# Joint products of k and v for two pairs of heads, with a remade order, in a linear-attention and feed-forward kernel

## The chip, the cores and the metric

The kernel runs on one core of a Trainium2 chip. The metric is the device time of one execution in microseconds (us). TensorE is called PE in the rows of the profile (its weight loads PEld), VectorE DVE, ScalarE ACT, GpSimd POOL and SyncE SP.

## The reference

A linear attention with softmaxes over q's rows and over the sequence of k is followed by a feed-forward net with a squared ReLU; all is float32. There are 8 batches of 8 heads, 576 positions and 64 columns a head; the net has 512 inputs and 2048 hidden units.

```python
q_s = exp(q - max(q, -1));  q_s = q_s / (sum(q_s, -1) + 1e-09)
k_s = exp(k - max(k, 2));   k_s = k_s / (sum(k_s, 2) + 1e-09)
kv = np.einsum('bhsd,bhse->bhde', k_s, v)
attn = np.einsum('bhsd,bhde->bhse', q_s, kv)
x = attn.transpose(0, 2, 1, 3).reshape(4608, 512)
g = np.maximum(x @ w_in, 0.0) ** 2
out = g @ w_out
```

## The kernel before

**Blocks and pairs.** A block is a batch: 512 of its 576 positions, the other 64 going to x_left for the end. Its eight heads are treated as four pairs, written b.pr; two heads of 64 columns fill the 128 partitions. A float32 product with full precision is made of three products of rounded parts (high by high, high by low, low by high), each with 512 moving columns; they are the bulk of PE's work. Blocks 0 to 2 go through the net step by step: one step is one slice of 128 hidden units of one block, with four groups of three products for the hidden layer (tokens h), relu, square, high and low part (relu, rm, ghi, glo), and four output tiles (tokens o). From block 3 on two blocks at a time go through a scheme with seven products (tokens s0, s1, s2; x0 to x2 prepare its inputs), whose weights come through a ring of tiles (tokens R).

**What sets the order.** Each engine runs its instructions in the order in which the kernel issues them. Two strings of tokens state that order: ORDER up to step 17, LIST from there to the end. `run` takes a token of LIST to a function; `kv/3.1` is the token kv of pair 1 of block 3. In LIST the attention of blocks 2 to 7 stands between the tokens of the net.

**The attention of one pair** (`attention`, from block 2 on). k's maximum is made and spread (km, k1, k2), subtracted (ke, on DVE) and exponentiated (kx, on ACT); q likewise (qm, qd, qx, qs, qy), then turned through DRAM (tb, Bw, B). Then come the tokens that the change touches:

- **kv**, on PE, is one *visit*: ten matmuls, five sequence slices of two heads, each 64 stationary columns (k) by 65 moving ones (v and a column of ones for the sum). One head's results go to partitions 0 to 63 of a PSUM bank, the other's to 64 to 127. The trace shows each matmul as two records, 20 to a visit, as `bank<-vt,kt`. With the changed and unchanged pairs there are 24 visits in blocks 2 to 7; for 2.0 and 2.1 they read another tile for k (`bank<-vt,ke`).
- **kr**, on DVE: 1e-9 added to the sum (rs), the reciprocal, and the scaling of the product (kf).
- **kh**, on ACT: the rounded high part is copied into the split operand kvs, by two copies of 64x64 in blocks 3 and 4 (THREE), by four in the others.
- **kl**, on DVE: two subtractions of 64x64 give the low part, also into kvs.
- **kz**, on POOL: two memsets, where kvs changes its layout (ahead of blocks 3 and 5).
- **P0 to P3**, on PE, multiply q by kvs (`bank<-qs,kvs`, 320 and 256 columns; in blocks 3 and 4 P0 and P1 of three matmuls each); **c** and **d** take them out of PSUM.

There are two split operands, used in turn by n % 2, where n counts the pairs; pairs 2.0 and 2.1 both use the first:

```python
kv_split = [const.tile([P, 2, P], F32R, name="kvs")]
kv_split.append(late.tile([P, 2, P], F32R, name="kvs1"))
kvs = kv_split[n % NB if two else 0]
```

The banks of kv and P come from next_bank: two in turn up to block 4, a single one after it.

Of the kernel before, what the change touches and what calls it, by code (L numbers as in the profile page):

```python
# [8 lines left out]
F32 = mybir.dt.float32  # L9
F32R = mybir.dt.float32r  # L10
# [86 lines left out]
kr/2.1 rm20 o.18.2 ke/2.2 kp/2.1 kh/2.1 B/2.2 o.18.3 k2/2.3 h21_0 ghi20 h21_1 kx/2.2 glo20 h21_2 w5.WA qs/2.3 h21_3
o.19.0 relu21 kl/2.1 o.19.1 ke/2.3 rm21 P0/2.1 w6.WA o.19.2 qm/3.0 qy/2.3 c0/2.1 o.19.3 kx/2.3 d0/2.1 h22_0 tb/2.3
ghi21 P1/2.1 h22_1 glo21 qd/3.0 Bw/2.3 c1/2.1 h22_2 d1/2.1 w7.WA qm/3.1 xh0/2.1 h22_3 xl0/2.1 P2/2.1 o.20.0 relu22
w0.a1 Lq/3.2 o.20.1 rm22 w0.s2 o.20.2 c2/2.1 qx/3.0 d2/2.1 XL/2.1 w0.s3 o.20.3 qs/3.0 P3/2.1 w0.s4 h23_0 ghi22  # L100
c3/2.1 h23_1 glo22 qh0/2.2 qy/3.0 h23_2 d3/2.1 h23_3 xh1/2.1 tb/3.0 xl1/2.1 kv/2.2 relu23 qm/3.2 Bw/3.0 ql0/2.2
# [20 lines left out]
ql0/3.3 h34_2 w3.h34 glo33 h34_3 st.1.1 w3.h12 qs/4.2 o.32.0 w3.l12 relu34 o.32.1 st.1.3 rm34 o.32.2 kx/3.3 w3.l34
w3.W12 o.32.3 qm/4.3 qy/4.2 kv/3.3 ghi34 w3.W34 h35_0 glo34 kp/3.3 Lk/4.1 h35_1 tb/4.2 h35_2 kr/3.3 qd/4.3 Lv/4.1
h35_3 k1/4.0 kh/3.3 o.33.0 relu35 w4.a2 o.33.1 k2/4.0 rm35 o.33.2 qx/4.3 B/4.0 w4.s1 o.33.3 qs/4.3 h36_0 ghi35 h36_1
glo35 qy/4.3 Lq/5.1 h36_2 km/4.1 h36_3 o.34.0 kl/3.3 x0.LB11 relu36 ke/4.0 o.34.1 Bw/4.2 rm36 P0/3.3 w4.a1 kx/4.0
o.34.2 tb/4.3 c0/3.3 w4.s2 o.34.3 back.0 w4.s3 k1/4.1 P1/3.3 ghi36 XL/3.3 h37_0 w4.s4 qh0/4.0 h37_1 glo36 c1/3.3
# [15 lines left out]
glo44 h45_3 ke/5.1 o.43.0 x0.LB22 relu45 tb/5.1 o.43.1 rm45 x0.T10 Bw/5.1 o.43.2 kx/5.1 o.43.3 x0.lB110 x0.hT10
h46_0 s0.R.1 ghi45 x0.lT10 h46_1 glo45 qd/5.2 h46_2 km/5.2 x0.hB220 h46_3 back.1 Lq/6.0 o.44.0 x0.T30 relu46 o.44.1
x0.T20 rm46 s0.R.2 o.44.2 x0.hT30 x0.T40 o.44.3 x0.hT20 x0.lT30 h47_0 ghi46 s0.R.3 x0.pB210 h47_1 x0.hT40 glo46
h47_2 x0.hB221 x0.lT20 qx/5.2 h47_3 x0.T11 o.45.0 s0.R.4 relu47 x0.lB111 o.45.1 rm47 x0.T31 o.45.2 x0.hT11 o.45.3
x0.hT31 x0.lT11 B/5.0 o.46.0 ghi47 x0.lT31 o.46.1 glo47 x0.pT40 o.46.2 s0.R.5 o.46.3 x0.T21 s0.0.A11 x0.T41 x0.hT21
x0.lT21 back.2 o.47.0 s0.0.c1 qs/5.2 x0.pB211 ev.2.0.a s0.0.S2 x0.hT41 st.2.0 k1/5.2 x0.pT41 s0.0.A12 s0.0.u2 s0.R.7
k2/5.2 qh0/5.0 x0.pB220 o.47.1 s0.0.r11 s0.0.S3 qh1/5.0 s0.0.m11 x0.pB221 back.3 ev.2.1.d s0.0.h0 s0.0.S1 s0.R.8
s0.0.u3 st.2.1 s0.0.l0 ql0/5.0 o.47.2 s0.0.a22 o.47.3 ev.2.2.a s0.0.A22 ql1/5.0 s0.R.6 s0.0.rf1 ev.2.3.d s0.0.qf1
qm/5.3 st.2.2 P0/5.0 s0.o.0.0 s0.0.r21 qy/5.2 c0/5.0 s0.o.0.1 s0.0.m21 s0.R.9 s0.o.0.2 d0/5.0 s0.0.h1 st.2.3  # L150
s0.o.0.3 s0.0.l1 P1/5.0 tb/5.2 s0.1.A11 s0.R.10 c1/5.0 d1/5.0 qd/5.3 Bw/5.2 s0.0.S4 qm/6.0 XL/5.0 s0.1.c1 ke/5.2
# [161 lines left out]
def attention_ffn_kernel(ctx: ExitStack, tc: tile.TileContext, q, k, v, w_in, w_out, out):  # L313
# [991 lines left out]
```

## Time and profile before

| | us |
|---|---|
| Median of 3 runs (lowest, highest) | 844.3 (843.94, 845.71) |
| The profiled execution, its own time | 843.6 |
| Its span, first to last instruction | 841.8 |
| PE busy | 833.6 |
| DVE busy | 550.4 |
| ACT busy | 494.3 |
| POOL busy | 288.4 |

The span lies 1.8 us under that execution's own time. Matmuls are pipelined, and their ends are modelled; the times from start to start tell the pace better than the durations. A few matmul records are missing from the trace. Nearly all instructions carry one line, L293, that of the helper that issues them, so groups are told apart by the tiles they write and read.

### The profile page before, as it was taken

What the parts mean: (1) busy time and instruction counts of PE and PEld (TensorE: products, weight loads), DVE (VectorE), ACT (ScalarE), POOL (GpSimd) and SP (SyncE); (2) the same over time, 40 slices, a digit from 0 to 9 for tenths busy, and PEclk for the clock granted to TensorE, in tenths of its full rate; (3) what the DMA queues carried; (4) which work ended last, traced back from release to release, by engine and by line L of the source; (5) the groups of instructions that cost most, each with busy time, mean ns of one, the idle gap of its engine ahead of it and who ended that gap; (6) DMA issues with size and microseconds to landing.
All of it is one profiled execution on the core that took longest, in us unless ns stands there. A gap on an engine that the chain in (4) does not pass through costs nothing.

```text
span 841.8 us, 13068 instructions
## 1 busy us (share of the span) xinstructions
PE 833.6 (99%) x4286; PEld 678.3 (81%) x4286; DVE 550.4 (65%) x1153; ACT 494.3 (59%) x934; POOL 288.4 (34%) x275
## 2 busy tenths in 40 slices
PE   8999999999999999999999999999999999999997
PEld 6778787878888888888887888888888888888886
DVE  7898888879988888668887896634348132222321
ACT  4889866677556656567667556566464244444411
POOL 4578654567776645244323143031002100000000
PEclk9999999999999999999999999999999999999999
DMA  9969987965777889988898837765576374554611
GB/s 238 274 182 301 255 289 231 325 189 174 215 225 239 238 252 273 271 240 277 243 252 260 286 113 233 231 202 181 174 236 186 100 225 151 160 170 151 183 62 50
DMA packets 156595, 179.66 MB, mean 213 GB/s; under 512 B 51696, under 2 KB 120304, under 8 KB 156528
## 3 DMA queue, kind: packets, MB, share of 16 engines
q1 hardware_dynamic: 155776, 177.88, 70.4%
q10 hardware_dynamic: 752, 0.95, 0.4%
q8 instruction: 34, 0.56, 0.3%
q14 instruction: 33, 0.27, 0.1%
HBM read 133.69 MB, written 45.09 MB: 212 GB/s over the span
## 4 chain that ended last, share of the span: by engine, by line
PE 84%; DVE 1%; issue 0%; ACT 0%; DVEq 0%; ACTq 0%
PE bank L293 84%; DVE w L293 0%; DVE bank L293 0%; DVE qn L293 0%; DVE r L293 0%; DVE g_lo L293 0%; DVE sums L293 0%; DVE o L293 0%; ACT bank L293 0%; ACT g_hi L293 0%; ACT wo L293 0%; DVE qs L293 0%; DVEq L293 0%; DVE tb L293 0%; ACTq L293 0%
## 5 line engine op out<-in xcount | busy, mean ns | idle before, releaser
L293 PE MATMUL bank<-wp,g 128*128 128x512 f32 x648 | 160.4, 390 | 0.0
L293 PEld LDWEIGHTS bank<-wp,g 128*128 128x128 f32 x648 | 120.6, 188 | 25.0
L293 PE MATMUL bank<-x_hi,wi 128*128 128x512 f32 x384 | 132.0, 398 | 0.0
L293 PE MATMUL bank<-xh_T,wp 128*128 128x512 f32 x384 | 131.8, 392 | 0.0
L293 PE MATMUL bank<-wo,g_hi 128*128 128x512 f32 x384 | 120.5, 395 | 0.0
L293 POOL TENSOR_TENSOR qs<-qT,qs 64x640 fp32r<-64x640 f32 (+1 forms) x40 | 64.0, 1599 | 101.1 <-ACT qs L293 92.7
L293 PE MATMUL bank<-xh_B,wp 128*128 128x512 f32 x288 | 97.2, 390 | 0.0
L293 DVE TENSOR_TENSOR c<-c,bank 128x512 f32<-128x512 f32 x48 | 33.0, 687 | 85.7 <-ACT c L293 85.6
L293 PEld LDWEIGHTS bank<-xh_T,wp 128*128 128x128 f32 x384 | 72.1, 188 | 16.4 <-ACT bank L293 0.8
L293 PEld LDWEIGHTS bank<-x_hi,wi 128*128 128x128 f32 x384 | 72.2, 188 | 16.2 <-DVE x_lo L293 0.4
L293 ACT ACTIVATE far<-far 128x512 f32<-128x512 f32 x96 | 60.5, 631 | 39.9 <-DVE far L293 38.5
L293 PEld LDWEIGHTS bank<-wo,g_hi 128*128 128x128 f32 x384 | 70.5, 188 | 15.0 <-ACT g_hi L293 0.4
L293 PE MATMUL bank<-wo,g_lo 128*128 128x512 f32 x192 | 75.1, 391 | 0.0
L293 PE MATMUL bank<-x_lo,wi 128*128 128x512 f32 x192 | 75.0, 391 | 0.0
L293 PE MATMUL bank<-xl_T,wp 128*128 128x512 f32 x192 | 74.9, 390 | 0.0
L293 PE MATMUL bank<-wo_back,g 128*128 128x512 f32 x288 | 72.2, 390 | 0.0
L293 DVE TENSOR_TENSOR far<-far,bank 128x512 f32<-128x512 f32 x48 | 33.0, 687 | 59.0 <-PE bank L293 58.3
L293 PEld LDWEIGHTS bank<-xh_B,wp 128*128 128x128 f32 x288 | 54.1, 188 | 11.5
L293 PEld LDWEIGHTS bank<-wo_back,g 128*128 128x128 f32 x288 | 53.5, 188 | 10.9
L293 DVE TENSOR_TENSOR g<-far,g 128x512 fp32r<-128x512 f32 x48 | 31.9, 703 | 41.7 <-ACT g L293 41.6
L293 POOL TENSOR_TENSOR qn<-qt,qm 128x640 f32<-128x640 f32 x30 | 40.0, 1337 | 53.3 <-DVE tb L293 31.8
L293 PE MATMUL bank<-xl_B,wp 128*128 128x512 f32 x144 | 56.2, 390 | 0.0
(135 smaller groups left out, 1519.9 us busy)
## 6 DMA issues: line engine op xcount, KB each, us to landing
wp<-w_outs SPq DMA_DIRECT2D x54, 512.0 KB, 4.4
wp<-w_sums SPq DMA_DIRECT2D x96, 256.0 KB, 3.6
wp<-w_own SPq DMA_DIRECT2D x72, 256.0 KB, 3.5
out_dram<-o SPq DMA_DIRECT2D x68, 128.0 KB, 2.6
raw_i<-in_moe_w_in_dram SPq DMA_DIRECT2D x16, 512.0 KB, 6.5
raw_o<-in_moe_w_out_dram SPq DMA_DIRECT2D x16, 512.0 KB, 7.5
bounce<-tb SPq DMA_DIRECT2D x24, 320.0 KB, 3.5
qT<-bounce SPq DMA_DIRECT2D x96, 80.0 KB, 3.0
```

Of the source, the lines that this page charges most:

```text
L293: ins = f(*args, **kwargs)
```

## The change

For pairs 0 and 1 of a block, and for pairs 2 and 3, the tokens kv, kr, kh, kl and kz are now one for both: a function `joint` holds them. Only 2.0 and 2.1 keep theirs. Both products go into one bank, 128 columns apart; kr, kh, kl and kz handle both pairs in one instruction each where they had one for each. The two operands are one tile, `[P, NB, 2, P]`, of the same size as both together; it is allocated and cleared at `late`, and the first one's clearing at the start of the kernel is gone. The products P0 to P3 of a pair read the pair's half of the tile. LIST is made anew from its first line on: 46 tokens fewer (2640, from 2686), none added, and the other tokens moved; its last lines are as before. ORDER is unchanged.

```diff
-    kv_split = [const.tile([P, 2, P], F32R, name="kvs")]
+    kv_split = []
...
     def attention(b, pr, two):
...
-        kvs = kv_split[n % NB if two else 0]
+        def kvs(*at):
+            return kv_split[0][:, pr % NB][at]
...
+    def joint(b, pr):
...
+        def kv():
+            ps = st["kv"] = next_bank("z" if b > THREE[-1] else "a")[:, : NB * P].rearrange("p (i f) -> p i f", i=NB)
+            for i in range(NB):
+                pairs[b, pr + i]["kvat"](ps[:, i, : D + 1])
+
+        def kr():
+            rs = attn_pool.tile([P, NB, 1], F32, name="rsj", tag="rsj")
+            e.dve.tensor_scalar_add(rs, st["kv"][:, :, D : D + 1], 1e-9)
+            e.dve.reciprocal(rs, rs)
+            st["kf"] = attn_pool.tile([P, NB, D], F32, name="kf", tag="kf0")
+            e.dve.tensor_tensor(st["kf"], st["kv"][:, :, :D], rs.broadcast_to([P, NB, D]), op=ALU.mult)
+
+        def kh():
+            kvs, kf = kv_split[0], st["kf"]
+            for h in range(2):
+                e.act.copy(kvs[half[h], :, 0, half[h]] if b in THREE else kvs[half[h], :, h, :D], kf[half[h]])
+            if b not in THREE:
+                for h in range(2):
+                    e.act.copy(kvs[half[1 - h], :, h, :D], kf[half[h]])
+
+        def kl():
+            kvs, kf = kv_split[0], st["kf"]
+            for h in range(2):
+                own = half[h]
+                lo, hi = (kvs[own, :, 1, own], kvs[own, :, 0, own]) if b in THREE else (
+                    kvs[own, :, h, D:], kvs[own, :, h, :D]
+                )
+                e.dve.tensor_tensor(lo, kf[own], hi.bitcast(F32), op=ALU.subtract)
...
-            kv_split.append(late.tile([P, 2, P], F32R, name="kvs1"))
-            clear(kv_split[1])
+            kv_split.append(late.tile([P, NB, 2, P], F32R, name="kvs"))
+            clear(kv_split[0])
...
-            pairs[int(b), int(args[0])][name]()
+            at = int(b), int(args[0])
+            if name in ("kv", "kr", "kz", "kh", "kl") and at not in ((2, 0), (2, 1)):
+                if at not in joints:
+                    joints[at] = joint(*at)
+                joints[at][name]()
+            else:
+                pairs[at][name]()
```

What the new LIST does is seen in the order of the instructions. On PE, before, around the visit of pair 4.0 (the row with vt0 and kt0; x_hi and wi belong to the hidden layer, x2 and x10 count like instructions):

```order
L293 MATMUL bank3_92<-x_hi0_75,wi5_739 128x512 x2
L293 MATMUL bank3_92<-x_lo0_76,wi5_739 128x512
L293 MATMUL bank3_92<-x_hi0_75,wi5_739 128x512
L293 MATMUL bank7_96<-vt0_87,kt0_78 64x65 x10
L293 MATMUL bank3_92<-x_hi0_75,wi5_739 128x512
L293 MATMUL bank3_92<-x_lo0_76,wi5_739 128x512
```

and further on around the visit of pair 4.1, 40 rows later:

```order
L293 MATMUL bank3_92<-x_hi0_75,wi7_925 128x512
L293 MATMUL bank3_92<-x_lo0_76,wi7_925 128x512
L293 MATMUL bank3_92<-x_hi0_75,wi7_925 128x512
L293 MATMUL bank0_89<-vt1_88,kt1_79 64x65 x10
L293 MATMUL bank3_92<-x_hi0_75,wi7_925 128x512
L293 MATMUL bank3_92<-x_lo0_76,wi7_925 128x512
```

Now, on PE, from the last products of pair 3.3 with the operand (qs, kvs) on:

```order
L290 MATMUL bank7_95<-qs0_2994,kvs_689 128x256
L290 MATMUL bank7_95<-qs1_3004,kvs_689 128x256
L290 MATMUL bank7_95<-qs0_2994,kvs_689 128x256
L290 MATMUL bank3_91<-x_hi0_75,wi5_736 128x512
L290 MATMUL bank3_91<-x_lo0_76,wi5_736 128x512
L290 MATMUL bank3_91<-x_hi0_75,wi5_736 128x512
L290 MATMUL bank2_90<-wo3_798,g_hi_2978 128x512 x2
L290 MATMUL bank2_90<-wo3_798,g_lo_2987 128x512
L290 MATMUL bank0_88<-vt0_86,kt0_78 64x65 x10
L290 MATMUL bank0_88<-vt1_87,kt1_79 64x65 x10
L290 MATMUL bank6_94<-wo3_798,g_hi_2978 128x512 x2
L290 MATMUL bank6_94<-wo3_798,g_lo_2987 128x512
```

The visit of 4.1 has moved up behind that of 4.0, and the operand that both will fill was last read five rows ahead of them; from the visit to the first product of pair 4.0 with the operand there are now 18 products of 512 columns.

On DVE, before, the work on the product of pair 3.0, with its neighbours (g_lo is the low part for the output layer, qm the maximum of q):

```order
L293 TENSOR_TENSOR g_lo_2430<-bank3_92,g_hi_2418 128x512
L293 TENSOR_SCALAR rs_2437<-bank7_96 128x1
L293 RECIPROCAL rs_2437<-rs_2437 128x1
L293 TENSOR_SCALAR kf_2440<-bank7_96,rs_2437 128x64
L293 TENSOR_REDUCE qm_2448<-qt0_80 128x10
L293 TENSOR_TENSOR kvs_84<-kf_2440,kvs_84 64x64 x2
```

and now that of pairs 3.0 and 3.1 together:

```order
L290 TENSOR_SCALAR rsj_2445<-bank0_88 128x2
L290 RECIPROCAL rsj_2445<-rsj_2445 128x2
L290 TENSOR_TENSOR kf_2448<-bank0_88,rsj_2445 128x128
L290 TENSOR_REDUCE sums0_692<-qn_2378 128x10
L290 TENSOR_REDUCE qs_2454<-sums0_692 128x10
L290 RECIPROCAL qs_2454<-qs_2454 128x10
L290 TENSOR_REDUCE qm_2469<-qt0_80 128x10
L290 TENSOR_TENSOR kvs_689<-kf_2448,kvs_689 64x2x64 x2
```

The scaling has become a product of two tensors, twice as wide, the subtractions are twice as wide, and q's sum now stands between the two.

## Rows read from the trace of the kernel before

**Rows 1.** The page: span, busy times and 40 slices (digits are tenths).

```profile
span 841.8 us, 13068 instructions
PE 833.6 (99%) x4286; PEld 678.3 (81%) x4286; DVE 550.4 (65%) x1153; ACT 494.3 (59%) x934; POOL 288.4 (34%) x275
...
PE   8999999999999999999999999999999999999997
...
PEclk9999999999999999999999999999999999999999
```

**Rows 2.** Chain that ended last, from 143 us on: start us, us, what.

```profile
142.84 694.14 PE bank L293 x3458
...
837.00 0.69 DVE o L293
```

**Rows 3.** Windows: us, busy of PE, PEld, DVE, ACT, POOL, clock, DMA share, GB/s.

```profile
185.50:327.40 141.90, 141.90 (x805) 115.99 (x803) 125.28 (x287) 89.12 (x181) 89.09 (x93) 1.00 0.76 224
327.40:500.00 172.60, 172.60 (x881) 140.61 (x880) 134.96 (x313) 113.40 (x215) 58.40 (x48) 1.00 0.84 248
```

**Rows 4.** Timeline of PE, one visit and a long stretch: start us, us, what.

```profile
267.84 0.39 PE L293 MATMUL bank<-x_hi,wi 128*128 128x512 f32 x1
268.16 0.80 PE L293 MATMUL bank<-vt,kt 128*64 128x65 f32 x20
268.89 0.50 PE L293 MATMUL bank<-x_hi,wi 128*128 128x512 f32 x1
269.23 0.40 PE L293 MATMUL bank<-x_lo,wi 128*128 128x512 f32 x1
...
809.61 5.60 PE L293 MATMUL bank<-wp,g 128*128 128x512 f32 x24
815.04 2.88 PE L293 MATMUL bank<-wo_back,g 128*128 128x512 f32 x12
```

**Rows 5.** Tile vt's products, and a visit's remaining records in two short windows.

```profile
L293 PE MATMUL bank<-vt,kt x440: 219/222/272, 170.8 to 579.3; 128*64 128x65 f32 x147
...
171.00 0.64 PE L293 MATMUL bank<-vt,kt 128*64 128x65 f32 x16
...
171.24 0.40 PE L293 MATMUL bank<-vt,kt 128*64 128x65 f32 x8
```

**Rows 6.** Timeline of PE in block 0: two groups in one visit.

```profile
25.48 0.80 PE L293 MATMUL bank<-vt,ke 128*64 128x64 f32 x20
26.11 0.70 PE L293 MATMUL bank<-ones,ke 128*64 128x1 f32 x20
26.74 0.66 PE L293 MATMUL bank<-ident,qn 128*128 128x128 f32 x4
```

**Rows 7.** Tiles rs and kvs: count, ns minimum/median/maximum, first and last start.

```profile
L293 DVE TENSOR_SCALAR rs<-bank x32: 118/155/160, 20.2 to 579.5; 128x1 f32<-128x1 f32 x32
L293 DVE RECIPROCAL rs<-rs x32: 161/164/166, 20.4 to 579.7; 128x1 f32<-128x1 f32 x32
L293 DVE TENSOR_SCALAR kf<-bank,rs x24: 263/284/285, 135.9 to 579.9; 128x64 f32<-128x64 f32 x24
...
L293 ACT CAST kvs<-kf x80: 232/243/248, 137.1 to 581.0; 64x64 fp32r<-64x64 f32 x80
L293 DVE TENSOR_TENSOR kvs<-kf,kvs x48: 154/222/1351, 137.4 to 584.0; 64x64 fp32r<-64x64 f32 x48
```

**Rows 8.** Timelines of ACT, PE and DVE where an input was ready late.

```profile
240.58 0.73 ACT L293 ACTIVATE kt<-kt 128x640 f32<-128x640 f32 x1
...
241.76 0.39 PE L293 MATMUL bank<-wo,g_lo 128*128 128x512 f32 x1
242.08 0.80 PE L293 MATMUL bank<-vt,kt 128*64 128x65 f32 x20
...
214.80 1.43 DVE L293 TENSOR_TENSOR kvs<-kf,kvs 64x64 fp32r<-64x64 f32 x2
...
216.25 0.60 PE L293 MATMUL bank<-qs,kvs 128*128 128x320 f32 x3
```

More of the change, by code (lines that the diff above doesn't have):

```diff
@@ L97 @@
[L97 to L101, printed above, removed]
@@ L122 @@
[L122 to L126, printed above, removed]
@@ L142 @@
[L142 to L151, printed above, removed]
@@ new lines @@
+relu30 w1.W34 o.28.1 rm30 ke/3.2 o.28.2 qh0/3.1 w1.W12 k1/3.3 o.28.3 kx/3.2 ql0/3.1 XL/3.0 h31_0 ghi30 k2/3.3 h31_1
+h31_2 B/3.2 w2.a2 glo30 P0/3.1 qs/3.3 h31_3 c0/3.1 w2.s1 o.29.0 relu31 XL/3.1 P1/3.1 ke/3.3 rm31 o.29.1 back.0
+qm/4.1 qy/3.3 kx/3.3 o.29.2 c1/3.1 o.29.3 XR/3.1 w2.s2 tb/3.3 kv/3.2 ghi31 qd/4.0 Bw/3.3 qh0/3.2 glo31 h32_0 Lv/4.1
+kr/3.2 w2.s3 qx/4.0 h32_1 kh/3.2 w2.s4 qs/4.0 h32_2 h32_3 kp/3.2 w2.h34 qy/4.0 o.30.0 Lq/4.2 relu32 o.30.1 rm32
+ql0/3.2 tb/4.0 o.30.2 w2.h12 Lk/4.0 o.30.3 h33_0 ghi32 w2.l34 kp/3.3 Bw/4.0 h33_1 Lk/4.1 glo32 qd/4.1 h33_2 qm/4.2
@@ new lines @@
+w7.s3 o.42.1 rm44 qm/5.3 o.42.2 w7.s4 k2/5.1 o.42.3 w7.h12 back.1 h45_0 ghi44 w7.l12 h45_1 w7.h34 glo44 h45_2 w7.l34
+w7.W12 h45_3 ke/5.1 w7.W34 o.43.0 relu45 qs/5.1 o.43.1 rm45 o.43.2 kx/5.1 qy/5.1 x0.LB22 o.43.3 kv/5.0 ghi45 s0.R.1
+glo45 x0.T10 h46_0 Lv/5.3 kp/5.0 kp/5.1 h46_1 x0.lB110 x0.hT10 h46_2 x0.lT10 h46_3 x0.T30 x0.hB220 o.44.0 s0.R.2
+x0.T20 relu46 o.44.1 rm46 x0.T40 Lk/5.2 o.44.2 x0.hT30 o.44.3 x0.hT20 x0.lT30 Lk/5.3 h47_0 ghi46 x0.lT20 h47_1
+x0.hT40 glo46 s0.R.3 h47_2 x0.hB221 x0.pT40 Lv/5.2 kr/5.0 h47_3 o.45.0 x0.T11 relu47 o.45.1 x0.lB111 rm47 o.45.2
@@ new lines @@
+x0.hT11 x0.T31 s0.R.4 o.45.3 x0.T21 x0.hT31 o.46.0 s0.R.5 ghi47 x0.lT11 o.46.1 x0.hT21 glo47 x0.pB210 o.46.2 kh/5.0
+o.46.3 x0.lT21 s0.0.A11 B/5.0 x0.T41 x0.lT31 x0.hT41 o.47.0 s0.0.c1 kl/5.0 km/5.2 x0.pB211 ev.2.0.a back.2 s0.0.S2
+st.2.0 tb/5.1 x0.pT41 s0.0.A12 s0.0.u2 s0.R.7 k1/5.2 qh0/5.0 x0.pB220 o.47.1 Bw/5.1 s0.0.r11 s0.0.S3 qh1/5.0
+s0.0.m11 x0.pB221 ev.2.1.d s0.0.h0 s0.0.S1 s0.R.8 s0.0.u3 st.2.1 s0.0.l0 ql0/5.0 o.47.2 s0.0.a22 o.47.3 ev.2.2.a
+s0.0.A22 ql1/5.0 s0.R.6 s0.0.rf1 ev.2.3.d s0.0.qf1 km/5.3 st.2.2 P0/5.0 s0.o.0.0 s0.0.r21 qd/5.2 s0.o.0.1 c0/5.0
@@ new lines @@
+qx/6.0 Lq/6.2 s0.2.A11 s0.1.l1 s0.1.qf1 ke/5.3 s0.R.15 s0.1.S4 s0.2.c1 qm/6.1 s0.R.14 kx/5.3 s0.o.3.0 qh0/5.1
+s0.1.a12 Bw/5.3 s0.2.S2 qs/6.0 qh1/5.1 ql0/5.1 s0.2.A12 s0.R.16 qm/6.2 s0.2.u2 ql1/5.1 s0.1.rf0 P0/5.1 s0.o.3.1
+s0.2.r11 qy/6.0 s0.2.S3 c0/5.1 s0.2.m11 B/5.2 d0/5.1 s0.2.h0 s0.2.S1 s0.2.l0 s0.2.u3 s0.R.17 s0.1.qf0 P1/5.1
+s0.o.3.2 s0.2.a22 c1/5.1 s0.o.3.3 d1/5.1 s0.2.rf1 back.3 tb/6.0 s0.2.A22 XL/5.1 s0.2.qf1 qd/6.1 Bw/6.0 P2/5.1
+s0.R.18 s0.o.4.0 s0.2.r21 s0.o.4.1 c2/5.1 s0.2.m21 Lq/6.3 s0.o.4.2 d2/5.1 s0.2.h1 P3/5.1 s0.2.l1 s0.o.4.3 c3/5.1
@@ new lines @@
+tb/6.3 s0.6.qf0 P3/6.1 s0.7.A12 qd/7.0 Bw/6.3 s0.7.u2 qh0/6.2 s0.o.13.1 Lq/7.2 c3/6.1 ql0/6.2 s0.7.r11 d3/6.1
+s0.7.S3 qh1/6.2 s0.7.m11 s0.R.40 ql1/6.2 XR/6.1 kv/6.2 s0.7.u3 s0.7.h0 s0.7.S1 x1.hB110 Lv/7.1 kp/6.2 kr/6.2 kp/6.3
+s0.7.l0 kh/6.2 s0.o.13.2 s0.o.13.3 x1.hB111 kl/6.2 s0.7.A22 s0.7.a22 s0.0.hf0 s0.R.39 s0.R.41 s0.0.lf0 s0.0.hf1
+Lk/7.1 P0/6.2 s0.o.14.0 s0.0.lf1 s0.7.r21 s0.o.14.1 c0/6.2 s0.7.m21 Lk/7.0 s0.o.14.2 d0/6.2 s0.7.h1 s0.o.14.3
+s0.7.rf1 s0.7.l1 Lv/7.0 P1/6.2 s0.7.S4 qm/7.2 c1/6.2 s0.7.qf1 d1/6.2 qx/7.0 s0.o.15.0 s0.7.a12 P2/6.2 s0.o.15.1
@@ new lines @@
+s1.o.19.3 x2.pT40 s1.o.20.0 s1.3.hf0 s1.o.20.1 s1.3.hf1 s1.3.lf0 s1.o.20.2 s1.3.lf1 s1.o.20.3 x2.T21 s1.o.21.0
+s2.R.0 x2.T41 x2.hT21 s1.o.21.1 x2.lT21 x2.hT41 s1.o.21.2 x2.lT31 s1.o.21.3 x2.pB210 s1.o.22.0 s1.4.hf0 s1.o.22.1
+s1.4.hf1 s1.4.lf0 s1.o.22.2 s1.4.lf1 s1.o.22.3 s1.o.23.0 x2.pB211 s2.R.1 s1.o.23.1 s1.o.23.2 x2.pT41 s1.o.23.3
+s1.o.24.0 x2.pB220 s1.5.hf0 s2.R.2 s1.o.24.1 s1.5.hf1 s1.o.24.2 s1.5.lf0 s1.o.24.3 s1.5.lf1 s1.o.25.0 x2.pB221
+s1.o.25.1 s1.o.25.2 s1.o.25.3 s1.o.26.0 s1.6.hf0 s2.R.3 s1.o.26.1 s1.6.hf1 s1.6.lf0 s1.o.26.2 s1.6.lf1 s1.o.26.3
@@ new lines @@
+s2.o.1.0 s2.R.10 s2.0.a12 s2.1.S2 s2.0.rf0 s2.0.qf0 s2.1.A12 s2.R.11 s2.1.u2 s2.o.1.1 s2.1.r11 s2.1.S3 s2.1.m11
+s2.R.12 s2.1.h0 s2.1.S1 s2.1.u3 s2.1.l0 s2.o.1.2 s2.R.13 s2.1.a22 s2.o.1.3 s2.1.rf1 s2.1.A22 s2.1.qf1 s2.o.2.0
+s2.1.r21 s2.o.2.1 s2.1.m21 s2.o.2.2 s2.1.h1 s2.o.2.3 s2.1.l1 s2.2.A11 s2.R.15 s2.1.S4 s2.2.c1 s2.R.14 s2.o.3.0
+s2.1.a12 s2.2.S2 s2.1.rf0 s2.1.qf0 s2.2.A12 s2.R.16 s2.2.u2 s2.o.3.1 s2.2.r11 s2.2.S3 s2.2.m11 s2.2.h0 s2.2.S1
+s2.R.17 s2.2.u3 s2.2.l0 s2.o.3.2 s2.2.a22 s2.o.3.3 s2.2.rf1 s2.2.A22 s2.2.qf1 s2.o.4.0 s2.R.18 s2.2.r21 s2.o.4.1
@@ new lines @@
+s2.2.m21 s2.o.4.2 s2.2.h1 s2.o.4.3 s2.2.l1 s2.3.A11 s2.R.19 s2.2.S4 s2.3.c1 s2.o.5.0 s2.R.20 s2.2.a12 s2.3.S2
+s2.2.rf0 s2.2.qf0 s2.3.A12 s2.3.u2 s2.o.5.1 s2.R.21 s2.3.r11 s2.3.S3 s2.3.m11 s2.3.h0 s2.3.S1 s2.3.u3 s2.3.l0
+s2.o.5.2 s2.R.22 s2.3.a22 s2.o.5.3 s2.3.rf1 s2.3.A22 s2.3.qf1 s2.o.6.0 s2.3.r21 s2.o.6.1 s2.3.m21 s2.o.6.2 s2.3.h1
+s2.o.6.3 s2.3.l1 s2.4.A11 s2.R.24 s2.3.S4 s2.4.c1 s2.R.23 s2.o.7.0 s2.3.a12 s2.4.S2 s2.3.rf0 s2.3.qf0 s2.4.A12
+s2.R.25 s2.4.u2 s2.o.7.1 s2.4.r11 s2.4.S3 s2.4.m11 s2.4.h0 s2.4.S1 s2.R.27 s2.4.u3 s2.4.l0 s2.o.7.2 s2.4.a22
@@ new lines @@
+s2.o.23.0 s2.o.23.1 s2.o.23.2 s2.o.23.3 s2.o.24.0 s2.5.hf0 s2.o.24.1 s2.5.hf1 s2.5.lf0 s2.o.24.2 s2.5.lf1 s2.o.24.3
+s2.o.25.0 s2.o.25.1 s2.o.25.2 s2.o.25.3 s2.o.26.0 s2.6.hf0 s2.o.26.1 s2.6.hf1 s2.6.lf0 s2.o.26.2 s2.6.lf1 s2.o.26.3
+s2.o.27.0 s2.o.27.1 s2.o.27.2 s2.o.27.3 s2.o.28.0 s2.7.hf0 s2.o.28.1 s2.7.hf1 s2.7.lf0 s2.o.28.2 s2.7.lf1 s2.o.28.3
+s2.o.29.0 s2.o.29.1 s2.o.29.2 s2.o.29.3 s2.o.30.0 s2.o.30.1 s2.o.30.2 s2.o.30.3 s2.o.31.0 s2.o.31.1 ev.8.0.a
+s2.o.31.2 st.8.0 ev.8.1.d s2.o.31.3 ev.8.2.a st.8.1 st.8.2 ev.8.3.d st.8.3
@@ L705, in kf @@
         def kf():
-            st["kf"] = attn_pool.tile([P, D], F32, name="kf", tag=f"kf{n % NB}")
+            st["kf"] = attn_pool.tile([P, NB, D], F32, name="kf", tag="kf0")[:, n % NB]
             e.dve.tensor_scalar_mul(st["kf"], st["kv"][:, :D], st["rs"])
-        def kv_clear():
-            z = kvs.bitcast(F32)
-            if b in THREE:
-                e.pool.memset(z[HALF:, :, :D], 0.0)
-                e.pool.memset(z[:HALF, :, D:], 0.0)
-            else:
-                e.pool.memset(z[HALF:, 0, D:], 0.0)
-                e.pool.memset(z[:HALF, 1, D:], 0.0)
         def kv_high():
-            if b in THREE:
-                for h in range(2):
-                    e.act.copy(kvs[half[h], 0, half[h]], st["kf"][half[h]])
-                return
             for h in range(2):
-                e.act.copy(kvs[half[h], h, :D], st["kf"][half[h]])
+                e.act.copy(kvs(half[h], h, slice(D)), st["kf"][half[h]])
             for h in range(2):
-                e.act.copy(kvs[half[1 - h], h, :D], st["kf"][half[h]])
+                e.act.copy(kvs(half[1 - h], h, slice(D)), st["kf"][half[h]])
         def kv_low():
             for h in range(2):
-                own = half[h]
-                if b in THREE:
-                    e.dve.tensor_tensor(
-                        kvs[own, 1, own], st["kf"][own], kvs[own, 0, own].bitcast(F32), op=ALU.subtract
-                    )
-                    continue
-                e.dve.tensor_tensor(kvs[own, h, D:], st["kf"][own], kvs[own, h, :D].bitcast(F32), op=ALU.subtract)
+                hi = kvs(half[h], h, slice(D)).bitcast(F32)
+                e.dve.tensor_tensor(kvs(half[h], h, slice(D, P)), st["kf"][half[h]], hi, op=ALU.subtract)
         def q_high(hs=(0, 1)):
@@ L789, in times @@
                 qs = st["q"][h][:, g0 : g0 + 2, :nj].rearrange("p g j a -> p g (j a)")
-                e.pe.matmul(view(st[key]).rearrange("p g j a -> p g (j a)"), kvs[:, h], qs, start=True, stop=True)
+                e.pe.matmul(view(st[key]).rearrange("p g j a -> p g (j a)"), kvs(slice(P), h), qs, start=True, stop=True)
             def copy():
@@ L815, in times @@
                     out = ps.rearrange("p (g f) -> p g f", g=2)
-                    e.pe.matmul(out, kvs[:, kl], qs, start=(i == 0), stop=(i == 2))
+                    e.pe.matmul(out, kvs(slice(P), kl), qs, start=(i == 0), stop=(i == 2))
             def copy():
@@ L868, in attention, with kz @@
         return fine, micro
+    def joint(b, pr):
+        sts = [pairs[b, pr + i]["st"] for i in range(NB)]
+        st = {}
+        def kv():
[8 more added lines that the diff above has]
+            e.dve.tensor_tensor(st["kf"], st["kv"][:, :, :D], rs.broadcast_to([P, NB, D]), op=ALU.mult)
+        def kz():
+            z = kv_split[0].bitcast(F32)
+            if b in THREE:
+                e.pool.memset(z[HALF:, :, :, :D], 0.0)
+                e.pool.memset(z[:HALF, :, :, D:], 0.0)
+            else:
+                e.pool.memset(z[HALF:, :, 0, D:], 0.0)
+                e.pool.memset(z[:HALF, :, 1, D:], 0.0)
+        def kh():
[13 more added lines that the diff above has]
+                e.dve.tensor_tensor(lo, kf[own], hi.bitcast(F32), op=ALU.subtract)
+        return dict(kv=kv, kr=kr, kz=kz, kh=kh, kl=kl)
     def h_part(ps, blk, fc, cc):
```

313 lines of the change are left out of this document (143 added, 170 removed).

## The prediction

> **What bounds the kernel now.** The page first: TensorE's matrix unit (PE) is busy for 833.6 of 841.8 us, and the granted clock stands at nine tenths or more in all 40 slices [rows 1]. A busy share alone proves little, so the chain of waits comes second, from step 17 on. It has three pieces, and the first is PE alone from 142.84 for 694.14 us; behind it stand one eviction and the last store [rows 2]. There is therefore no other engine to relieve there: only PE's own stream can become shorter, or be interrupted. The windows come third: while the attention steps run, VectorE (DVE) is busy for 125.28 of 141.90 us, then for 134.96 of 172.60, and the clock is 1.00, the upper level of 2.4 GHz [rows 3]. DVE is behind PE, but not far behind.
>
> The question is then at what price PE does its work. In a long unmixed stretch 24 products of 512 columns take 815.04 - 809.61 = 5.43 us, 0.226 each [rows 4]. One visit for the product of k and v breaks that pace: the last 512-column product ahead of it starts at 267.84, the 20 records of the visit at 268.16 (0.32 later, not 0.23), the next 512-column product at 268.89, and the one behind that only at 269.23, 0.34 later [rows 4]. From 267.84 to 269.23 are 1.39 us, in which two 512-column products would have taken 0.45. **One visit costs 0.94 us.** There are 440 records of this kind, 20 to a visit, so 22 visits [rows 5], and none stands next to another.
>
> **The change part by part.** *The visits.* The number of matmuls stays. Eleven times, two visits become one of 40 records, so eleven times the second group of 20 runs without a way in and a way out. What such a group costs inside a visit is read from the steady part: cut at two places, the same visit has 16 records left from 171.00 and 8 from 171.24, so 8 records take 0.24 us, 0.03 each, and 20 take 0.60, with the rounding 0.58 to 0.62 [rows 5]. Bounds: below, 0.58; above, a group that carries one edge of a visit, the first of a pair of groups that already stand in one visit in the first block: 25.48 to 26.11, 0.63, and the second 26.11 to 26.74, 0.63 with the way out [rows 6]. That pair is also the nearest row for the seam between two groups: the second follows at the pace of the first, with no step. I take 0.59, near the steady part. A merge then saves 0.94 - 0.59 = 0.35 us (0.31 to 0.36), and eleven save 3.85, say **3.8 us** (3.4 to 4.0).
>
> *The operations between a visit and its products.* On DVE a pair has one addition (0.15), one reciprocal (0.16), one scaling (0.28) and two subtractions of 0.22; on ScalarE (ACT) two or four copies of 0.24 [rows 7]. Eleven times the second pair's set goes, and the remaining ones are twice as wide: the scaling becomes a product of 128x128. No row has its form. It is bounded below by the 0.28 of half the width and above by the 0.69 of the last eviction, which reads a whole bank of 128x512 [rows 2, 7]; I take 0.35, near the lower end, since it is a quarter of that bank. If all wider ones cost nothing extra, DVE gets back 11 x 1.03 = 11 us, if they cost double, nothing. Of this nothing reaches the end, because PE waits for neither engine [rows 2]: counted as zero. The cover is the room ahead of the first product, and its loss is the third rival below. The memsets of the operand (POOL) become fewer; the two at the start go, and the clearing behind them is not what PE's first transposes waited for; zero too.
>
> *The single operand.* Before, two operands alternate, and a pair's split is written while the pair ahead is still being multiplied. Now both pairs of a group lie in one, its next writing (ACT's copies) waits for the last product of the group ahead, and behind the copies on ACT are queued the rounding copies for the hidden layer, for which PE waits. At the first group of block 4 the order has those last products, five further rows, the visit, and then 18 products of 512 columns (18 x 0.226 = 4.1 us) to the group's first product. The chain in between is 0.15 + 0.16 + 0.35 + 2 x 0.24 + 2 x 0.22 = 1.6 us [rows 7], with wider copies and subtractions at most 2.5. It fits: zero.
>
> *The second pair's exponential.* The visit now starts when both pairs are ready. The tightest wait that the trace shows had ACT's exponential end at 241.31 and the visit begin at 242.08, and the way in is not longer there than elsewhere (241.76 to 242.08, 0.32) [rows 8]. The new order leaves one set of three 512-column products between the second exponential and the visit at four of the eleven; nothing speaks for a wait, and each 0.1 us of it would cost 0.1.
>
> *The order.* The remade list moves most attention steps by some microseconds, weight refills by less. The trace shows that PE follows such a list for 694 us without a stop [rows 2]; for the new one that isn't known. I leave it at zero and put it into the range: half a microsecond better (a few products of q with the operand start late in the trace of before) to a few worse.
>
> **Sum.** Profiled execution: 841.8 of span and 1.8 around it are 843.6; less 3.8 gives 839.8 (span 838.0). The median of the three runs, 844.3, lies 0.7 above that execution, and what is measured will be a median again: 844.3 - 3.8 = **840.5 us**, 0.45% faster. A measurement of this kernel can tell about 0.2%, 1.7 us, from no change.
>
> **The rivals.**
> 1. *The order gives back a part.* Small waits of 1 to 2 us in all, where DVE has little left [rows 3]: 841.5 to 842.5. Against it: the piece of 694 us. Chance 0.10, still faster.
> 2. *Only the way in is saved.* The late first 512-column product and the 0.34 behind it could belong to each group of short products rather than to the visit; then a merge saves 0.32 - 0.23 = 0.09 us [rows 4], eleven save 1.0, and the time is 843.3, no change that can be told. For it: the two effects can't be separated in any row of a single visit. Against it: in the visits with two groups the second starts without a step [rows 6]. Chance 0.10. The Trainium skill (TensorEngine Tiling (Array Packing), Key Properties) says that changing the tiling mode drains TensorE, which fits the way in. By TensorE: Matmul & The Clock Gate (Step-by-step: what each phase is for) a drain is about 128 cycles; by that figure, as an estimate from that page, two changes at 2.4 GHz would be 0.11 us a visit and the sum 843.1. The row of a visit shows 0.35, and it decides.
> 3. *Slower: the wide subtractions come late.* In blocks 3 and 4 DVE is 88% busy [rows 3], and there a pair of subtractions, 64 columns wide, once took 1.43 us instead of 0.44, while PE's product followed at once (214.80 + 1.43 = 216.23, product at 216.25) [rows 8]. If they take twice that for two pairs, PE stands for 1.4 us at each of the five groups of blocks 2 to 4: 7.0 - 3.8 = 3.2 us, 847.5. It decides from four groups on (5.6 - 3.8 = 1.8). For it: with one operand the split can't be written ahead. Against it: the room of 4.1 us above. Chance 0.08.
> 4. *The change doesn't do what it says*: the order has all eleven groups of 20 behind one another on PE, with nothing between; only a wait at the seam could part them. Chance 0.02, no change.
>
> **How the numbers follow.** The forecast has 0.70. Faster by over 0.2% are the forecast and rival 1, 0.80; within are rivals 2 and 4, 0.12; slower is rival 3, 0.08. The range: below, 4.0 us for the merges, 0.5 from the order and 0.9 for the scatter of the medians (the profiled execution lies 0.7 under the median), so 844.3 - 5.4 = 838.9; above, it reaches through rival 1 and stops just short of rival 2, 842.7.
>
> **What would show it.** Right: visits of 40 records, 1.3 us from first record to the next 512-column product (0.73 + 0.59), eleven of them; 0.32 on the way in and 0.34 behind, once each; span near 838.0; the chain still one piece of PE, near 690.3 us from 142.84. Wrong: a step between the 20th and the 21st record; idle time of PE released by ACT or DVE ahead of a visit or of a product of q with the operand (rivals 1 and 3, rival 3 with subtractions near 1.4 us each); a late refill of weights would be an error of the order that I have not priced apart.

## The result, and the profile after

The changed kernel takes 850.9 us (median of 6 runs, 850.20 to 851.51), the kernel before 844.12 in the same comparison (6 runs, 843.32 to 845.71): a ratio of 1.0079 (95% interval 1.0066 to 1.0092). It is slower by 6.7 us by that ratio (6.8 between the two medians), and above the whole predicted range. The page of the profiled execution, which answers to [rows 1] (digits are tenths):

```profile
span 849.0 us, 12969 instructions
PE 840.7 (99%) x4286; PEld 678.0 (80%) x4286; DVE 538.4 (63%) x1098; ACT 487.2 (57%) x898; POOL 288.1 (34%) x269
...
PE   8999999999999999999999999999999999999997
...
PEclk9999999999999999999999999999999999999999
```

PE has as many records as before, 4286, and the clock stands at nine tenths or more in all slices, as before. The 7.2 us by which the span grew are not idle time: PE's busy time rose by 7.1. The chain of waits from 143 us on (start, duration, what), which answers to [rows 2]:

```profile
142.85 19.80 PE bank L290 x103
...
193.86 1.58 POOL qs L290
195.48 648.72 PE bank L290 x3178
```

It still is PE's own stream. What cuts it at 195 is one small wait: a product of q with the operand, ahead of which the chain has POOL's part of q, starts 0.45 us after the 512-column product at 195.03 instead of some 0.23. The visits, which answer to [rows 4] (timeline of PE: start, duration, records):

```profile
201.28 0.39 PE L290 MATMUL bank<-x_hi,wi 128*128 128x512 f32 x1
201.59 1.39 PE L290 MATMUL bank<-vt,kt 128*64 128x65 f32 x40
202.91 0.50 PE L290 MATMUL bank<-x_hi,wi 128*128 128x512 f32 x1
203.25 0.40 PE L290 MATMUL bank<-x_lo,wi 128*128 128x512 f32 x1
```

There are the 40 records, with 0.31 on the way in, 1.32 from the first record to the next 512-column product, and 0.34 behind that, once. Eleven visits are alike to 0.01 us. So the change does what it says, the path is still PE alone, and yet PE needs longer. What is new is seen in the long stretch near the end, where nothing was changed:

```profile
810.44 2.96 PE L290 MATMUL bank<-wp,g 128*128 128x512 f32 x12
813.24 2.96 PE L290 MATMUL bank<-wo,g 128*128 128x512 f32 x12
```

Twelve products take 813.24 - 810.44 = 2.80 us, 0.233 each, against 0.226 in [rows 4]. Worked out over all neighbouring 512-column products of the two traces (3163 before, 3190 after, start to start), the mean rose from 227.5 to 231.2 ns; 3.7 ns for some 3,180 of them are 11.7 us; less the 3.9 us that the eleven merged visits save in the same traces, that leaves 7.8, near the 7.2 by which the span grew. The products are slower from the first steps on, where the order is the same as before, and not for all tiles alike: products of xh_T with wp stay at 227 to 229, those of wp with g rise to 233.4.

### The profile page after: what moved, and what is told of

Same layout as the page of the kernel before. It is cut to its first block, busy times and chain, and to the rows that moved or that the text cites. A ratio compares the mean times of both kernels' runs of the same rounds, so it can differ in the third digit from the quotient of the medians.

```text
span 849.0 us, 12969 instructions
## 1 busy us (share of the span) xinstructions
PE 840.7 (99%) x4286; PEld 678.0 (80%) x4286; DVE 538.4 (63%) x1098; ACT 487.2 (57%) x898; POOL 288.1 (34%) x269
## 4 chain that ended last, share of the span: by engine, by line
PE 90%; DVE 3%; DMA 3%; issue 1%; SPq 1%; ACT 1%; POOL 1%; DVEq 0%; POOLq 0%; ACTq 0%
PE bank L290 90%; DMA raw_o<-in_moe_w_out_dram 1%; DVE m L290 1%; DMA qt<-in_q_dram 1%; DMA kt<-in_k_dram 1%; SPq L290 1%; DMA raw_i<-in_moe_w_in_dram 0%; POOL qs L290 0%; DVE g_lo L290 0%; DVE bank L290 0%; DVE w L290 0%; DVE ke L290 0%; DVE xf L290 0%; DVE qs L290 0%; DVE qm L290 0%
## 5 line engine op out<-in xcount | busy, mean ns | idle before, releaser
L290 PE MATMUL bank<-wp,g 128*128 128x512 f32 x648 | 164.7, 395 | 0.0
L290 PE MATMUL bank<-wo,g_hi 128*128 128x512 f32 x384 | 122.3, 399 | 0.0
L290 DVE TENSOR_TENSOR g<-far,g 128x512 fp32r<-128x512 f32 x48 | 33.9, 745 | 48.2 <-ACT g L290 48.1
L290 PEld LDWEIGHTS bank<-xh_B,wp 128*128 128x128 f32 x288 | 54.1, 188 | 11.7
L290 POOL TENSOR_TENSOR qn<-qn,qs 128x640 f32<-128x640 f32 x30 | 37.8, 1262 | 72.4 <-DVE qs L290 56.2
L290 ACT CAST g<-far 128x512 fp32r<-128x512 f32 x48 | 27.6, 620 | 54.1 <-PE bank L290 53.9
```

The costliest lines, as they stand in the source:

```text
L290: ins = f(*args, **kwargs)
```

## The experiments

**What the theory was.** Neither engines nor the order of the work differ in that stretch; what differs is where the tiles lie. The first split operand was 1,024 bytes a partition ahead of the other tiles, and the new small tile rsj takes 32, with its own tag. So the tiles behind both moved by 992 bytes, the weights (wi, wo, wp; xh and xl too) from byte 80512 to 79520, and g_hi, which lies between the two, by 1,024, from 40576 to 39552, whereas the tile g of the later stages, which shares its place with x_hi of the first, stayed at 1152. These places are those that the program assigns; no view of the profile shows them. A product reads a moving operand and a stationary one, and its row names the moving one first: in `wp,g` the weight moves and g is stationary, in `x_hi,wi` x_hi moves and the weight is stationary. Before, these tiles all started at the same place within 512 bytes (1152, 40576 and 80512 all leave 128). After, g, g_hi and x_hi are 32 bytes apart from the weights; xh_T and wp, both moved by the same 992 bytes, are not apart. Theory A: the distance between the two operands sets PE's pace. Rival B: the joint operand or the new order slows PE.

**e3: the shift alone, in the kernel before.** Two operands, separate visits and the old order, and one unused tile of 32 bytes ahead of the weights:

```diff
+    w_pool.tile([P, 8], F32, name="shift", bufs=1)
```

> The kernel before, with an unused tile of 32 bytes ahead of the work tiles: two operands and the old order, but the weights' tiles at 32 within 64 bytes and x_hi0, g and g_hi at 0, as in the changed kernel. Theory A: some 2000 products of different phase at 233.3 instead of 227.5 ns, 11 to 12 us more, 855 us (853 to 857). Rival B: the shift does nothing, 844.1 us.

Measured: 856.5 us (854.97 to 858.03), 1.0143 of before (1.0121 to 1.0164). The timeline of PE:

```profile
803.65 5.76 PE L293 MATMUL bank<-wp,g 128*128 128x512 f32 x24
809.25 2.96 PE L293 MATMUL bank<-wo_back,g 128*128 128x512 f32 x12
```

24 products take 5.60 us, 0.233 each, and the mean over all neighbouring 512-column products is 231.2 ns, as in the changed kernel. The time lies in the range of theory A. 32 bytes of nothing cost the old kernel 12.1 us; the joint visits and the order are not needed for that. And beside a kernel with the same shift the change is a gain: 850.9 against 856.5.

**e1, e2 and e4: the changed kernel with other distances.** Each has an unused tile ahead of the weights, of 96 bytes (e1) or 32 (e2), and e4 has 32 there and 32 more ahead of all tiles, so that both operands move:

```diff
+    w_pool.tile([P, 24], F32, name="shift", bufs=1)
```

> The changed kernel with one unused tile of 96 bytes a partition ahead of the work tiles, so that every operand of TensorE starts at a multiple of 128 bytes again; instructions and order unchanged. Theory A (in the changed kernel moving and stationary tiles stand at different places within 64 bytes, 992 bytes of shift, and such a 512-column product takes 233 ns from start to start instead of 227): the products go back to 227, and the time is 844.1 - 3.8 = 840.3 us, 839.5 to 841.5. Rival B (the joint visits or the remade order slow PE): nothing changes, 850.9 us.

> The changed kernel with an unused tile of 32 bytes instead: the tiles of the weights then stand at 64 within 128 bytes, those of x_hi0, g and g_hi at 0. Theory A, with 64 bytes as the unit: 840.3 us as in the run with 96 bytes. If the unit is 128 bytes or more: about 851 us, products of different phase at 233 ns. Rival B: 850.9 us whatever the shift.

> The changed kernel with 32 bytes ahead of everything and 32 ahead of the work tiles: all operands of TensorE at 32 within 64 bytes, so all of one phase but none at a multiple of 64. Theory A (what counts is that moving and stationary differ): 840.3 us, products at 227 ns. Rival C (what counts is a start at a multiple of 64 bytes, for either operand): slower than the changed kernel, 853 us or more, since now every product has both operands off it. Rival B: 850.9 us.

Measured: e1 850.85 us (ratio 1.0076, 1.0061 to 1.0091), e2 844.88 (1.0009, 0.9994 to 1.0024), e4 845.35 (1.0015, 1.0003 to 1.0027). The timeline of PE in e1:

```profile
805.41 2.96 PE L290 MATMUL bank<-wp,g 128*128 128x512 f32 x12
808.21 2.96 PE L290 MATMUL bank<-wo_back,g 128*128 128x512 f32 x12
```

and in e2:

```profile
801.20 2.91 PE L290 MATMUL bank<-wp,g 128*128 128x512 f32 x12
803.95 2.91 PE L290 MATMUL bank<-wo_back,g 128*128 128x512 f32 x12
```

2.80 us for twelve in e1, 2.75 in e2. None of the three came out at 840.3: e1 stayed where rival B had it, e2 and e4 fell between 840.3 and 850.9, which rival B doesn't allow, since they keep the joint visits and the new order, and e4 stayed below the 853 of rival C. So my first form of theory A fell too: at a distance of 128 bytes, a multiple of 64, nothing is mended; at 64 bytes the pace is 229 ns for wp with g, and x_hi with wi stays at 232. e2 and e4 have one distance at two places, and their paces are the same, 229.4 for wp with g in both: the distance counts, not the place. Left was that only the distance 0 is free.

**e6: the change without its shift.** The small tile takes a slot of the pool that is there already, and the weights come to lie at 79488, the same place within 512 bytes as g:

```diff
-            rs = attn_pool.tile([P, NB, 1], F32, name="rsj", tag="rsj")
+            rs = attn_pool.tile([P, NB, 1], F32, name="rsj", tag="rs1")
```

> The changed kernel with one edit: the small tile of reciprocals takes the slot of another of the same size, so that the weight tiles start 32 bytes lower, at 79488 instead of 79520, which is again the same place within 512 bytes as the moving tiles (before: 80512; 80512 and 79488 both leave 128). Theory A' (the pace of the 512-column products follows from the distance, modulo 512 bytes, between where the moving and the stationary operand lie; at distance 0 it is 227 ns, at 32 it is 233): the pace returns to 227 everywhere, what the merged visits save remains, and the time is 840.3 us (839.5 to 841.5), the forecast of the change without its shift. Rival B (part of the 6.7 us belongs to the joint operand or to the new order): the pace returns to 227, but the time stays above 842, between 842 and 846. Rival C (the distance isn't what matters): as the changed kernel, 850.9.

Measured: 839.17 us, 0.9947 of before (0.9931 to 0.9964), that is 5.1 us faster than 844.26 (interval 3.0 to 5.8). The page, the chain and two rows of PE's timeline:

```profile
span 837.3 us, 12969 instructions
PE 828.6 (99%) x4286; PEld 679.1 (81%) x4286; DVE 539.4 (64%) x1098; ACT 486.6 (58%) x898; POOL 288.3 (34%) x269
```

```profile
193.03 1.57 POOL qs L290
...
194.65 637.82 PE bank L290 x3178
```

```profile
799.65 2.88 PE L290 MATMUL bank<-wp,g 128*128 128x512 f32 x12
802.37 2.88 PE L290 MATMUL bank<-wo,g 128*128 128x512 f32 x12
```

The last piece of the chain has the same 3178 records as in the changed kernel and takes 637.82 us instead of 648.72: 10.9 us for 32 bytes. The time is in the range of theory A' and below the 842 to 846 of rival B. Twelve products take 2.72, 0.227 each. The small wait behind POOL's part of q is there as well, so it was no part of the loss. The costliest groups of PE show the same on the page (busy time, mean ns of one); of the changed kernel:

```profile
L290 PE MATMUL bank<-wp,g 128*128 128x512 f32 x648 | 164.7, 395 | 0.0
...
L290 PE MATMUL bank<-x_hi,wi 128*128 128x512 f32 x384 | 132.9, 400 | 0.0
L290 PE MATMUL bank<-xh_T,wp 128*128 128x512 f32 x384 | 131.4, 392 | 0.0
```

and of e6:

```profile
L290 PE MATMUL bank<-wp,g 128*128 128x512 f32 x648 | 160.7, 390 | 0.0
...
L290 PE MATMUL bank<-x_hi,wi 128*128 128x512 f32 x384 | 131.3, 396 | 0.0
L290 PE MATMUL bank<-xh_T,wp 128*128 128x512 f32 x384 | 130.8, 391 | 0.0
```

One group rises by 5 ns, one by 4, one by 1: a rise of a per cent in the mean of one group while its neighbour stands still is how this cause looks on a page. The version beats both kernels.

**e5: the visits apart again, at the good distance.** As e6, with the second pair's products issued as a visit of their own behind the next piece of PE's work (a new token kw in LIST):

```diff
-            for i in range(NB):
-                pairs[b, pr + i]["kvat"](ps[:, i, : D + 1])
+            pairs[b, pr]["kvat"](ps[:, 0, : D + 1])
+
+        def kw():
+            pairs[b, pr + 1]["kvat"](st["kv"][:, 1, : D + 1])
```

> As e6_joint_same_phase, with one further edit: in each of the eleven groups the second pair's twenty products leave the joint visit and are issued behind the next piece of work of TensorE, a visit of their own; operand, operations and order of all else stay. Prices by the forecast: 0.35 us for each visit that is a separate one again, eleven of them 3.8 us, so 844.1 us (843.5 to 844.7), if the neighbour work has 512 columns. If a merge saves only the way in (0.09 each): 1.0 us above e6_joint_same_phase. If the merge saves nothing: the same time as it.

Measured: 845.79 us (1.0018 of before, 1.0005 to 1.0030), 6.6 above e6, where 3.8 were forecast. The timeline of PE:

```profile
201.46 0.39 PE L289 MATMUL bank<-x_hi,wi 128*128 128x512 f32 x1
201.78 0.80 PE L289 MATMUL bank<-vt,kt 128*64 128x65 f32 x20
202.51 0.51 PE L289 MATMUL bank<-x_hi,wi 128*128 128x512 f32 x1
202.85 0.40 PE L289 MATMUL bank<-x_lo,wi 128*128 128x512 f32 x1
203.09 0.40 PE L289 MATMUL bank<-x_hi,wi 128*128 128x512 f32 x1
203.42 0.80 PE L289 MATMUL bank<-vt,kt 128*64 128x65 f32 x20
```

and the longest wait in its view of waits that e6's has not (us in total, times, longest):

```profile
PE bank L289 <- DVE kvs L289: 1.1, 2, 0.9
```

The way in, 0.32, and the 0.34 behind are paid twice. Summed over the trace, as the prediction counted it (from the product ahead to the second one behind, less two products of 0.2267), the 22 visits cost 0.941 each, 20.7 us; e6's eleven cost 1.519 each, 16.7. That is 4.0 us, 0.36 a merge. The other 2.6 stand at the products of q with the operand: summed over the two traces from the product ahead to the second one behind, these cost 2.5 us more in e5. 1.3 of it are at the two places where PE waits for DVE's split (0.84 and 0.47 us longer than in e6; the view gives 1.1 of idle time there): here the joint operations begin only when the second visit is done, nearer to the products that read them. 0.47 more are at one place behind a wait for xf, and the rest is spread over seven places at up to 0.17 us each, whose cause I don't know.

**m1 and m2: PE alone.** These two hold only products and leave the whole computation out. In m1 one moving tile runs against stationary slices whose starts step by 32 bytes.

> Only products of 512 columns, nothing of the reference's computation: one moving tile of two rows of 2048 bytes (start 128 within 512 bytes) against 16 stationary slices of 512 bytes whose starts step by 32 bytes through all of 512 (sa 128, sb 160, sc 192 and so on), 48 products each; then the first slice shifted by 4, 8 and 16 bytes, 48 each with 8 of another slice behind; then the 16 again with a moving tile whose second row lies 32 further; then the first again. Theory A' expects 226 to 227 ns for sa, about 233 for sb and sp (32 off to either side), 229 to 232 for 64 off, 232 to 233 for 128 off, values in between for the rest, and a rise already at offsets under 32. If the distance is only a mark of something else in the kernel (other engines that write meanwhile), all 16 run at one pace, near 226.

The timeline of PE (each row one slice):

```profile
23.76 10.37 PE L45 MATMUL bank<-mv,sa 128*128 128x512 f32 x45
33.97 11.35 PE L45 MATMUL bank<-mv,sb 128*128 128x512 f32 x48
45.16 11.36 PE L45 MATMUL bank<-mv,sc 128*128 128x512 f32 x48
56.36 11.40 PE L45 MATMUL bank<-mv,sd 128*128 128x512 f32 x48
67.60 11.32 PE L45 MATMUL bank<-mv,se 128*128 128x512 f32 x48
78.75 11.37 PE L45 MATMUL bank<-mv,sf 128*128 128x512 f32 x48
89.96 11.16 PE L45 MATMUL bank<-mv,sg 128*128 128x512 f32 x48
100.95 11.36 PE L45 MATMUL bank<-mv,sh 128*128 128x512 f32 x48
112.15 11.05 PE L45 MATMUL bank<-mv,si 128*128 128x512 f32 x48
123.03 11.35 PE L45 MATMUL bank<-mv,sj 128*128 128x512 f32 x48
```

From start to start, by 48: sb 233 ns, sc 233, sd 234, se 232, sf 233, sg 229, sh 233; then si, 256 bytes behind sa, 227, as sa itself (10.21 us for 45); and sj as sb. In the window from 24 to 204 us, in which these rows lie, no other engine is busy and the granted clock is 1.00. A start moved by only 4, 8 or 16 bytes gives 232, 231 and 233 (at 4 bytes 48 products from 201.22 to 212.38). So the loss belongs to PE's two operands and needs no other engine, and the free distances are the multiples of 256, and not only those of 512, as theory A' had it. The direction counts as well: sc, whose start is 64 bytes above that of the moving tile, takes 233, and sg, 64 below it modulo 256, takes 229. That agrees with e2 and e4: there the stationary wi stands 64 above the moving x_hi (232), and the stationary g 64 below the moving wp (229). The Trainium skill (SBUF — State Buffer, SBUF: two separate sides) says that on the engines' side only the port pair that VectorE shares with GpSimd causes contention and that PE never waits on anyone. m1 can't test a wait for another engine, since none is busy in it; what it shows, 227 against 233 ns by the places of PE's own two operands, is a loss that this sentence does not name.

**e7: the period in the kernel.** As e6, with the unused tile ahead of g_hi 256 bytes shorter, so that the distance from g to the weights is 256 bytes off what it was (`PAD = 24` for 88).

> As e6_joint_same_phase, with one number changed: the unused tile ahead of the hidden tiles is 256 bytes shorter (24 instead of 88 words), so that the weights lie at 79232 and the hidden tiles at 39296, both 256 bytes lower, while the tile g of the later stages stays at 1152. Distance between the moving g (and the x of the first stage) and the weights then 256 instead of 0 modulo 512; modulo 256 it stays 0. Theory A'' (period 256, as m1_phases shows with its slice si): pace 227 everywhere, 839.2 us as e6_joint_same_phase (838.2 to 840.5). Theory A' (period 512, the size of a stationary slice): the products on g and on x_hi, some 1,600 of them, run 2 to 6 ns longer, 842.5 to 849.

Measured: 839.41 us (838.85 to 840.48), 0.9947 of before (0.9931 to 0.9964), with 227.2 ns for wp with g. The period of 256 bytes holds in the kernel. (The expectation calls g moving; in `wp,g` it is the stationary one, and the distance is the same.)

**m2: what of the two operands.**

> Only products, nothing of the reference's computation. In this order: 64 and 48 of 512 columns with moving m0 and stationary sa (distance 0 modulo 256); 48 with m0 and sb (32); 96 with m0 and sa, sb in turn; 48 with a moving tile that lies 32 further and sb (0 again, other place); 48 with it and sa (32 the other way); 96 with m0 and it in turn on sb; 96 that pair m0 with sa and the other tile with sb in turn (each product has distance 0, but against the stationary operand that is loaded meanwhile 32); then 384 columns with sa and with sb, 256 columns with sa and with sb, 48 each; at the end 48 of 512 with sa. Theory D (the product's own two operands decide): 226.7 for each pair at distance 0, the last mixed group included, and 230 as the mean of the group that takes sa and sb in turn. Theory E (the moving operand of one product collides with the stationary operand that is loaded for the next while it runs): the mixed group of pairs at distance 0 runs at about 233, and sa, sb in turn on m0 at a mean of 230. If the cost is one per product, 384 and 256 columns with sb lose the same 6.6 ns; if it is one per column, 5 and 3.3 ns.

The rows that answer it (timeline of PE; mv and mw are the moving tiles m0 and the one 32 bytes further):

```profile
45.07 0.40 PE L46 MATMUL bank<-mv,sa 128*128 128x512 f32 x1
...
67.63 11.07 PE L46 MATMUL bank<-mw,sb 128*128 128x512 f32 x48
78.54 11.35 PE L46 MATMUL bank<-mw,sa 128*128 128x512 f32 x48
89.73 0.40 PE L46 MATMUL bank<-mv,sb 128*128 128x512 f32 x1
...
111.83 0.39 PE L46 MATMUL bank<-mv,sa 128*128 128x512 f32 x1
...
134.07 8.51 PE L46 MATMUL bank<-mv,sa 128*128 128x384 f32 x48
142.42 8.49 PE L46 MATMUL bank<-mv,sb 128*128 128x384 f32 x48
150.74 5.92 PE L46 MATMUL bank<-mv,sa 128*128 128x256 f32 x48
156.50 5.83 PE L46 MATMUL bank<-mv,sb 128*128 128x256 f32 x48
```

Both operands moved by 32 run at (78.54 - 67.63) / 48 = 227 ns, one of them at 233. But from 111.83 to 134.07 pairs at distance 0 take turns at two places, and their mean is 22.24 / 96 = 232 ns: theory D, that only a product's own two operands count, falls. Theory E expected 233 there, but also a mean of 230 where sa and sb take turns on one moving tile, and that group (96 products from 45.07 to 67.63) took 235. Neither fits. A third group narrows it: with the two moving tiles in turn on the one slice sb (89.73 to 111.83) the mean is 230, as both theories have it. So what theory D lacks shows only where two stationary slices 32 bytes apart take turns, and there it is 5 ns in both groups (235 for 230, 232 for 227). And with 384 or 256 columns the distance of 32 costs nothing (173 against 174 ns, 118 against 120, the last 48 ending at 162.17): the cost is neither one per product nor one per column. By what mechanism the two reads meet is open.

## Why the prediction was wrong, point by point

- **The visits**: right. 0.35 us for a merge were forecast; the traces show 2 x 0.937 - 1.519 = 0.355, 3.9 us for eleven against 3.8. The step of 20 records more was taken as 0.59; it is 1.318 - 0.734 = 0.58. Rival 2, that only the way in is saved, fell: both edges are paid once, and with e5 twice.
- **The wider operations**: right that they cost next to nothing, but with less room than was worked out. The trace of e6 has 0.291 for the scaling (taken as 0.35), 0.297 for a double copy and 0.290 for a double subtraction in the median (count, ns minimum/median/maximum), and beside it the timelines of DVE and PE at the first group of block 3:

```profile
L290 DVE TENSOR_TENSOR kvs<-kf,kvs x26: 223/290/1375, 137.2 to 556.7; 64x128 fp32r<-64x128 f32 x22, 64x64 fp32r<-64x64 f32 x4
...
204.62 2.28 DVE L290 TENSOR_TENSOR kvs<-kf,kvs 64x128 fp32r<-64x128 f32 x2
...
206.92 0.60 PE L290 MATMUL bank<-qs,kvs 128*128 128x320 f32 x3
```

  The slow pairs of subtractions that rival 3 feared did come: 2.28 us here, 2.67 at 325.15, near its doubled 2.86. The prediction's bound of 2.5 us for the whole chain was therefore too low: here it took 4.75, from 202.15 to 206.90. The products that read the operand start at 206.92, in step with those ahead of them, so the room held, but with nothing to spare. One product of q (178.41, in block 2) starts 0.22 us late, and e6's view of waits has no wait for DVE's split: rival 3 named the right sign, but its mechanism cost PE about 0.2 us and not 7.0.
- **The second exponential**: right at zero; the way in is 0.32 at all eleven.
- **The order**: right at near zero. One wait of some 0.2 us behind POOL's part of q is new, and rival 1's 1 to 2 us did not come.
- **The single operand**: here the prediction failed. It asked of that step whether the next writing fits, and it did. But that the first operand left its place ahead of all other tiles, and that a tile of eight bytes came in with a tag of its own, stood in the same diff and was given no price; and the sum took for granted that the other 3,000 products would keep the pace of the trace of before. The term left out, 32 bytes of shift, measured +12.1 us in the kernel before (e3) and +11.7 in the changed one (850.9 less e6's 839.2); the removal of 1,024 bytes, four times 256, does no harm by itself. No rival covered it: two looked for idle time of PE, two for a smaller saving at the visits, and the time went into the pace of products that the change does not touch.
- **The sum without that term**: 840.5 forecast, 839.2 measured in e6, inside the predicted range. The change as it was meant gains; the changed kernel as it stands loses more than twice as much through its memory plan.

## What to carry to other kernels

A diff that adds, removes or resizes any tile moves the tiles behind it: work out the new places of PE's operands before pricing anything else, and if a kernel was tuned at one placement, keep the distances between its moving and stationary tiles, here modulo 256 bytes. If the busy time of the bounding engine grows with the number of its instructions unchanged and the clock at its upper level, compare the pace from start to start of one untouched group in both traces, before looking for a wait. A change should be judged at the placement of the kernel that it is compared with, or else at the best placement of each: at equal distances this one was worth 5.1 us (e6 against before) and 5.6 us (after against e3), and at its own it looked like a loss.

## What the runs showed of the hardware

PE's pace for products of 512 columns of these rounded float32 operands depends on where its two operands start in a partition: 227 ns when the starts are equal modulo 256 bytes, 229 to 234 otherwise (m1), with 4 bytes off already enough for 232. PE alone shows it, at 384 and 256 columns it is absent (m2), and two pairs that are each well placed but 32 bytes apart from one another still take 232 in turns.
